# Two edge columns on ScalarE are tied behind the large copies beside them, in the spectral stage of a gated-mix gradient kernel

## The chip, the core and the metric

The kernel runs on one core of one Trainium2 chip. The metric is the device time of one execution in microseconds (us). Five engines work from queues of their own: PE (TensorE, matrix products), DVE (VectorE), ACT (ScalarE), POOL (GpSimd) and SP (SyncE, which here only starts transfers). ACT and POOL start transfers too. Every queue is worked off in the order in which it was written: an instruction that waits for a semaphore holds up all that stands behind it on its engine.

## What is computed

The reference, cut to what matters:

```python
g = sigmoid((x * gate_w).sum(-1, keepdims=True))
a = irfft2(rfft2(x) * (w_r + 1j * w_i), s=(S, D))      # spectral filter
r = relu(x @ w1 + b1);  b = (r * r) @ w2 + b2           # squared-ReLU layer
out = g * a + (1 - g) * b
```

with S = 2048 rows, D = 1024 columns and 3584 hidden units. Outputs are `out` and the gradients of everything but the second input, for a given `grad_out`: nine arrays. Two of them, `out_2` and `out_3`, are the gradients of the filter's real and imaginary part, 2048 x 513 each: 512 ordinary columns and one at the edge of the half spectrum.

## The kernel before, in words

Two streams of work are woven into one program. The first is the dense layer: `mlp_in` computes the hidden values (matrix products of lines L811 and L919) and, by `back_` and `grads`, the gradient at the hidden values (L818); `mlp_grads` then computes the weight gradients (L1241), and `Outputs` the output and the gradient of x (L1540). The second is the spectral filter: `first_stage`, `fft_mid` and `fft_out`. `spread` deals steps of the second stream between steps of the first, so PE gets an order in which both are mixed. A tile framework then orders the instructions of each engine by its own cost estimates and by the dependencies that it sees: instructions that touch the same elements stay in order, instructions that touch different elements of a tile may pass one another. `after(ins, earlier, NoSync)` adds a dependency by hand: `ins` must stand behind `earlier` on the same engine, without a semaphore.

The change lies in `fft_mid`, which runs from about 225 us to 615 us of the span. Its loop goes over m = 0 to 15; each m handles two of the 32 residue classes of the row index (64 rows each) in two halves of 256 columns, h = 1 first and then h = 0. In one m:

- `spectra` (L434): PE makes `px` for both halves from the loaded `z`.
- `transform` (L438 to L442): ACT copies `px` into the tile `x` (L439, 128x1024), writes its negative (L440, 128x512), and then writes one edge column of x from the small tile `ex` (L441, 128x6). The edge column is column 0 for h = 0, and column 256 for h = 1, behind the 256 that L439 and L440 write. After the h = 1 half, ACT starts four transfers of the next `z` (L404), tied behind L440.
- `products` (L449), `joined` (L454, L457, L461) and `grads_of_w` (L494, L495) on DVE: the filtered spectrum `y` and, in `gs`, the products for the filter's gradient.
- `rows_of` (L468, PE), `copy_of` (L475, ACT, into the single buffer `vc`) and `back` (L482, L483, DVE; stores to `y_scr` by L485 on POOL).
- `grads_out` for m - 1 (L498 to L508): for each half ACT scales `gs` into the bfloat16 tile `gw` (L499, 128x512, tied behind the second L440 of this m), and then one edge column of `gw` (L504, 128x2). That is column 0 for h = 0, and column 512 for h = 1. When both halves are written, POOL starts four stores of `gw` to `out_2` and `out_3` (L508). `gw` has one buffer: the first write into it for one m has to wait until the four stores of the m before have landed.

For h = 0 the edge column overlaps the columns of the large write, so it has always stood behind it. For h = 1 it lies beside them, and the framework was free to place L441 and L504 ahead of the large writes. In the order of the program before it does: L504 for h = 1 is placed as soon as `gs` is there, 9 to 27 us ahead of its L499, and it is there that the semaphores of the four stores are waited for.

On ACT the same queue holds the dense layer's work: copies of PSUM banks (L923), ReLU (L933, L936), squares (L786). PE cannot write the next product into a bank of `ph` before ACT's L923 or L933 (or DVE's L935) has read it, and cannot write `pd` before DVE's L822 has read it.

Of the kernel before, what the change touches and what calls it, by code (L numbers as in the profile page):

```python
# [21 lines left out]
def pair_of(m, R1):  # L22
    return (m, R1 - m) if m else (0, R1 // 2)
# [118 lines left out]
def kernel(  # L142
# [22 lines left out]
    nc = tc.nc  # L165
# [10 lines left out]
    Q, H, LW, W1 = D // 4, D // 2, g.Df + 1, g.Df  # L176
# [4 lines left out]
    GS = 2.0 / (S * D * XS * XS)  # L181
# [46 lines left out]
    HW, HL = H // 2, P // 2  # L228
# [21 lines left out]
    def after(ins, earlier, wait=mybir.DependencyClass.Sync):  # L250

        if earlier is not None:
            info = mybir.DependencyInfo(wait, mybir.DependencyReason.DATA)
            tc.add_manual_dep(ins.ins, earlier.ins.name, info, reason="paced")
# [78 lines left out]
    def fft_mid(filler):  # L333
# [103 lines left out]
        def transform(m, h, px, ex):  # L437
            x = fb.tile([P, 3, 2, WL], FDT, name="x", tag="x", bufs=2)  # L438
            nc.scalar.copy(out=x[:, 1:3, :, 0:HW], in_=px[:])  # L439
            copied = nc.scalar.mul(out=x[:, 0, :, 0:HW], in_=px[:, 1], mul=-1.0)  # L440
            nc.scalar.copy(out=x[:, :, :, h * HW], in_=ex[:, m, :, :, h])  # L441
            return x, copied  # L442

        def products(h, x, w):
# [53 lines left out]
        def grads_out(m, h, gs, gw, done):  # L498
            main = nc.scalar.mul(  # L499
                out=gw[:, :, h * HW : (h + 1) * HW].rearrange("p c (i g) -> p c i g", g=4),  # L500
                in_=gs[:, :, 0:HW].rearrange("p c (g i) -> p c i g", g=4), mul=GS,
            )
            after(main, done, mybir.DependencyClass.NoSync)
            nc.scalar.mul(out=gw[:, :, h * H], in_=gs[:, :, h * HW], mul=0.5 * GS)  # L504
            if h == 0:
                for c_, dst_w in enumerate((out_2, out_3)):
                    for n, k in enumerate(pair_of(m, R1)):
                        st(out=every(dst_w, k), in_=gw[lanes[n], c_, 0:W1])  # L508
# [8 lines left out]
        ex = edges_through(ams)  # L517
# [5 lines left out]
        x, y, gs, was = {}, {}, {}, None  # L523
        yield
        for m in range(NM):
            more = m + 1 < NM
            px = {h: spectra(m, pm[h]) for h in (1, 0)}
            if m:
                gs[0], _ = grads_of_w(0, x[0])
            x[1], copied = transform(m, 1, px[1], ex)  # L530
            if more:
                z = {h: inputs(m + 1, h, copied) for h in (1, 0)}
            yield
            x[0], done = transform(m, 0, px[0], ex)
            yield
            tt = products(1, x[1], w[1])
            if m:
                gw = fb.tile([P, 2, LW], BF16, name="gw", tag="gw")
                for h in (1, 0):
                    grads_out(m - 1, h, gs[h], gw, done)  # L540
# [31 lines left out]
        gw = fb.tile([P, 2, LW], BF16, name="gw", tag="gw")  # L572
        for h in (1, 0):
            pv = rows_of(NM - 1, y[h])
            vc = copy_of(NM - 1, pv)
            yield
            back(NM - 1, h, pv, vc)
            grads_out(NM - 1, h, gs[h], gw, vc[1])
            yield
# [1336 lines left out]
    out = later["out"]  # L1916
# [36 lines left out]
```

## Time and profile before

| | |
|---|---|
| median of 3 runs | 1206.56 us (1205.56 to 1207.74) |
| the profiled execution: its own time | 1211.84 us |
| the profiled execution: span from the first to the last instruction | 1210.1 us |
| PE busy in the span | 1176.1 us (97%) |
| DVE, ACT, POOL busy | 892.5 us (74%), 528.5 us (44%), 377.6 us (31%) |
| mean granted TensorE clock | 0.999 |
| from 250 to 465 us (215 us, the dense layer's first part beside `fft_mid`): PE, DVE, ACT busy | 197.11, 174.56, 142.24 us |
| from 500 to 600 us (weight gradients beside `fft_mid`): PE busy | 99.58 us |

"Busy" is the share of time in which an instruction of that engine ran; idle time that is put down to a releaser ("<-") is the time in which an engine's next instruction waited, and the releaser is what came last. The profile's own execution lies 5.28 us above the median of the timed runs, so differences are read within the profile and then carried to the median.

### The profile page before, as it was taken

The page shows a single profiled execution, that of the slowest core. Times are in us where ns is not written, and L with a number is a line of the kernel's source. Part 1 is how long each engine was busy: PE and PEld are TensorE (multiplying, and loading weights), DVE is VectorE, ACT ScalarE, POOL GpSimd, SP SyncE. Part 2 cuts the span into 40 slices and gives each one's busy share as a digit, 9 for nine tenths or more (in the row PEclk, how much of TensorE's full clock was granted, in tenths as well). Part 3 has the DMA queues.
Part 4 walks back from the last instruction along what each step waited for, and adds up shares of the span by engine and source line. Part 5 has one row for each costly group of instructions (what it writes and reads, how often), then busy time and mean ns, then how long its engine had stood idle before and what let it go on. Part 6 is the DMA issues. An engine that isn't in the chain of part 4 may idle for free.

```text
span 1210.1 us, 19414 instructions
## 1 busy us (share of the span) xinstructions
PE 1176.1 (97%) x7181; PEld 639.9 (53%) x7275; DVE 892.5 (74%) x1598; ACT 528.5 (44%) x961; POOL 377.6 (31%) x618
## 2 busy tenths in 40 slices
PE   9999999998989989999999999999999999999998
PEld 5555555443433333444445999999644444444444
DVE  6888887778878776877546666766786577986757
ACT  5668788586666674344322666665201010000000
POOL 0233443656656764455241223231101100000000
PEclk9999999999999999999999999999999999999999
DMA  9997675796868677889998999994788999664530
GB/s 277 268 304 210 190 203 161 211 236 155 216 156 200 223 189 221 177 181 228 217 198 167 207 244 227 266 236 150 238 177 243 256 270 282 199 187 152 175 126 35
DMA packets 329464, 249.84 MB, mean 206 GB/s; under 512 B 187912, under 2 KB 287658, under 8 KB 328858
## 3 DMA queue, kind: packets, MB, share of 16 engines
q1 hardware_dynamic: 268352, 112.12, 43.8%
q0 software_dynamic: 35136, 111.72, 29.4%
q10 hardware_dynamic: 25882, 24.76, 6.9%
q8 instruction: 57, 0.93, 0.3%
q14 instruction: 37, 0.30, 0.1%
HBM read 114.82 MB, written 89.67 MB: 169 GB/s over the span
## 4 chain that ended last, share of the span: by engine, by line
PE 69%; DVE 14%; ACT 6%; DMA 5%; issue 4%; POOL 1%; ACTq 1%; another core or an unknown queue 0%; SPq 0%; DVEq 0%; POOLq 0%
PE pX L1241 15%; PE xX L1540 13%; PE pV L1241 11%; PE pd L818 7%; PE xV L1540 6%; PE ph L919 5%; PE xZ L1540 3%; DMA out_dram<-gw 3%; PE pui L325 1%; DMA dhT_scr<-dhT 1%; DVE dhT L822 1%; PE pki L626 1%; ACT gw L499 1%; DVE rT L935 1%; PE pu L325 1%
## 5 line engine op out<-in xcount | busy, mean ns | idle before, releaser
L818 PE MATMUL pd<-dbT,w2T 128*128 128x512 bf16 x860 | 208.4, 380 | 7.5 <-DVE dhT L822 5.3
L818 PEld LDWEIGHTS <-w2T 128*128 128x128 bf16 x896 | 86.3, 98 | 109.5 <-issue 10.6
L822 DVE SCALAR_TENSOR_TENSOR dhT<-pd,rT 128x512 bf16<-128x512 f32 x112 | 76.7, 685 | 46.9 <-PE pd L818 43.0
L1540 PEld LDWEIGHTS <-dS 128*128 128x128 f16 x686 | 66.4, 98 | 79.4 <-issue 3.7
L1591 POOL DMA_DIRECT2D out_dram<-ot x32 | 17.3, 542 | 244.6 <-DVE ot L1647 128.0
L1657 ACT ACTIVATE w2br<-w2br,dsc 128x512 f32<-128x512 bf16 x8 | 5.8, 723 | 175.6 <-DVE ot L1647 117.4
L1540 PE MATMUL xX<-oT,dS 128*128 128x512 f16 x336 | 76.4, 379 | 0.6 <-DVE eR L1569 0.5
L1257 ACT COPY u<-pX 128x512 f32<-128x512 f32 x56 | 32.8, 585 | 95.7 <-PE pX L1241 89.8
L1540 PEld LDWEIGHTS <-odd 128*128 128x128 bf16 (+1 forms) x462 | 44.8, 98 | 51.5 <-issue 0.9
L1540 PEld LDWEIGHTS <-even 128*128 128x128 bf16 (+1 forms) x448 | 43.6, 98 | 52.6 <-issue 0.7
L1241 PEld LDWEIGHTS <-T 128*128 128x128 f16 x672 | 64.6, 98 | 7.5 <-issue 0.2
L485 POOL DMA_DIRECT2D y_scr<-pc x64 | 46.1, 722 | 65.5 <-DVE pc L482 44.0
L936 ACT ACTIVATE rT<-rT 128x512 bf16<-128x512 bf16 x69 | 43.4, 630 | 37.7 <-DVE rT L935 37.6
L786 ACT ACTIVATE h2T<-rT 128x1024 bf16<-128x1024 bf16 x56 | 59.5, 1063 | 0.2
L1261 DVE TENSOR_TENSOR whi<-pV,u 128x512 bf16<-128x512 f32 x28 | 19.3, 689 | 48.4 <-ACT u L1257 48.3
L1241 PEld LDWEIGHTS <-S 128*128 128x128 f16 x336 | 32.6, 98 | 40.5 <-DVE S L1173 1.9
L449 DVE TENSOR_TENSOR tt<-x,w 128x1028 f16<-128x1028 f16 (+1 forms) x64 | 42.1, 689 | 7.3 <-ACT x L439 3.5
L1241 PEld LDWEIGHTS <-resL 128*128 128x128 bf16 x448 | 43.0, 98 | 4.9
L1241 PEld LDWEIGHTS <-resR 128*128 128x128 f16 (+1 forms) x448 | 42.9, 98 | 4.9 <-issue 0.2
L1261 DVE TENSOR_TENSOR wlo<-pV,u 128x512 bf16<-128x512 f32 x28 | 19.2, 686 | 34.4 <-PE pV L1241 34.2
L919 PEld LDWEIGHTS <-w1g 128*128 128x128 bf16 x252 | 23.9, 98 | 37.8 <-issue 11.9
L1241 PEld LDWEIGHTS <-even 128*128 128x128 bf16 (+1 forms) x256 | 24.5, 98 | 32.7 <-issue 2.1
(382 smaller groups left out, 2782.3 us busy)
## 6 DMA issues: line engine op xcount, KB each, us to landing
h2T_scr<-h2T POOLq DMA_DIRECT2D x28, 512.0 KB, 4.6
dhT_scr<-dhT POOLq DMA_DIRECT2D x28, 512.0 KB, 4.6
y_scr<-pc POOLq DMA_DIRECT2D x64, 128.0 KB, 4.4
ax_scr<-yo POOLq DMA_DIRECT2D x16, 512.0 KB, 5.3
out_dram<-ot POOLq DMA_DIRECT2D x31, 256.0 KB, 3.4
z<-z_scr ACTq DMA_DIRECT2D x60, 128.0 KB, 4.3
out_dram<-whi POOLq DMA_DIRECT2D x28, 256.0 KB, 5.4
out_dram<-wlo POOLq DMA_DIRECT2D x28, 256.0 KB, 5.2
```

The costliest lines, as they stand in the source:

```text
L325: first_ = mm(pu[:, bank, lo : lo + n], lhsT=ft[:, b, :], rhs=mat[:, o : o + n], start=bool(f_ & 1), stop=bool(f_ & 2), skip_group_check=True,
L449: V(out=tt[:, k, :, :, 0:W], in0=x[:, a : a + 2, :, 0:W], in1=by, op=ALU.mult)
L485: st(out=columns_of(y_scr, c, h), in_=pc[:, n])
L786: after(nc.scalar.activation(h2T, rT, ACT.Square), behind_, mybir.DependencyClass.NoSync)
L818: mm(pd[:], lhsT=w_[:, ec, fc % FGC * P : (fc % FGC + 1) * P], rhs=dbT[:, ec, ss], start=(ec == 0), stop=(ec == DC - 1),)
L822: return STT(out=dhT, in0=pd[:], scalar=2.0, in1=rT, op0=ALU.mult, op1=ALU.mult, accum_out=gb1part[:, fc, sb : sb + 1],)
L919: mm(acc[:], lhsT=lhs[:, t, :], rhs=rhs[:, t, :], start=start and t == 0, stop=t == KH - 1, skip_group_check=True)
L936: nc.scalar.activation(rT, rT, ACT.Relu)
L1241: self.mm = mm(out, lhsT=lhs[:, t, m * P : (m + 1) * P], rhs=rhs[:, t, :], start=start and t + a == 0, stop=t == KH - 1, skip_group_check= ...
L1257: turn["ACT"] = nc.scalar.copy(out=t_[:], in_=self.X[:])
L1261: turn["DVE"] = self.added = V(out=self.half(row, j), in0=self.sums(acc), in1=self.sums(t_), op=ALU.add)
L1540: ins = mm(acc, lhsT=lhs[:, fc, :], rhs=rhs[:, fc, :], start=start and fc == 0, stop=fc == KH - 1 and bias is None, skip_group_check=True,)
```

## The change

Two dependencies are added, both within ACT and without a semaphore. The edge column of x stands behind the two large copies of x of the same half (L439, L440), and the edge column of `gw` stands behind the large write of `gw` of the same half (L499). No instruction is added or taken away, and no shape, buffer or transfer changes.

```diff
             copied = nc.scalar.mul(out=x[:, 0, :, 0:HW], in_=px[:, 1], mul=-1.0)
-            nc.scalar.copy(out=x[:, :, :, h * HW], in_=ex[:, m, :, :, h])
+            after(nc.scalar.copy(out=x[:, :, :, h * HW], in_=ex[:, m, :, :, h]), copied, mybir.DependencyClass.NoSync)
             return x, copied
...
             after(main, done, mybir.DependencyClass.NoSync)
-            nc.scalar.mul(out=gw[:, :, h * H], in_=gs[:, :, h * HW], mul=0.5 * GS)
+            edge_ = nc.scalar.mul(out=gw[:, :, h * H], in_=gs[:, :, h * HW], mul=0.5 * GS)
+            after(edge_, main, mybir.DependencyClass.NoSync)
             if h == 0:
```

The line numbers here and below are those of the kernel before; in the kernel after, every line from L505 on is one higher.

In the order of the built program the h = 1 column of x moves behind its L440 and ahead of the four starts of `z` (L404); the h = 1 column of `gw` moves behind its L499, and the wait for the four stores moves with the tile's first write to that L499. As the framework orders anew around them, some neighbours change places: on DVE, `y` (L454) and the ReLU's sum (L935) swap in several m, and `pc` (L482, L483) moves up; on ACT, in three of the m, the second copy into `vc` (L475) moves from behind L933 to ahead of it. PE's order changes in a few places by a few products; POOL's stores keep their order but for small moves, and SP's queue is unchanged.

## The prediction

> **What bounds the kernel now.** I read first the page's busy times with the slices, then the windows of 10 us over the stage that the change touches, then the waits of ACT and PE in that stage, and last the timelines of ACT and PE around single gaps.
>
> ```profile
> PE 1176.1 (97%) x7181; PEld 639.9 (53%) x7275; DVE 892.5 (74%) x1598; ACT 528.5 (44%) x961; POOL 377.6 (31%) x618
> PE   9999999998989989999999999999999999999998
> ```
>
> PE bounds the kernel: 1176.1 of 1210.1 us. All that an edit of order can win is in the 34.0 us in which PE is idle, and the slices below 9 put most of that in the third of the span where `fft_mid` runs beside the dense layer. The windows give it as numbers (columns: PE, PEld, DVE, ACT, POOL busy, then clock, DMA share and GB/s):
>
> ```profile
> 300.00:310.00 10.00, 7.32 (x38) 3.14 (x38) 8.08 (x14) 5.64 (x10) 3.79 (x5) 1.00 1.09 241
> 350.00:360.00 10.00, 7.87 (x33) 3.02 (x29) 6.76 (x15) 6.71 (x11) 6.23 (x10) 0.83 0.65 145
> 510.00:520.00 10.00, 9.95 (x51) 4.26 (x50) 8.38 (x16) 3.04 (x7) 4.29 (x8) 1.00 1.00 184
> ```
>
> From 250 to 465 us PE is busy for 197.11 of 215 us, so 17.9 us are idle. From 490 us on, beside the weight gradients, every window has 9.95 or 10.00: there `fft_mid` goes on and nothing is to be won. So the change is worth what it does between 250 and 465 us. Next, who made ACT and PE wait between 225 and 625 us (total us, times, longest):
>
> ```profile
> ACT gw L504 <- DMA out_dram<-gw: 32.1, 12, 4.2
> ACT gw L504 <- DVE pm L425: 5.2, 2, 3.3
> ACT gw L504 <- DVE pc L483: 3.4, 1, 3.4
> ...
> PE pd L818 <- DVE dhT L822: 5.3, 5, 2.1
> PE ph L919 <- ACT rT L933: 4.7, 2, 2.7
> PE ph L919 <- ACT cu L923: 3.1, 2, 1.9
> PE ph L919 <- ACT u L923: 2.0, 2, 1.2
> ```
>
> ACT stands still at the early edge column of `gw` 15 times, once for every m that has a predecessor: 32.1 + 5.2 + 3.4 = 40.7 us. The two DVE names are, I think, the same thing: at 321.00 `gs` had been ready since 316.7, while the four stores were started from 316.25 to 318.35 and land within 2.4 to 8.3 us. The timelines of ACT and PE show what one such stop does:
>
> ```profile
> 297.44 0.63 ACT L936 ACTIVATE rT<-rT 128x512 bf16<-128x512 bf16 x1 [0.63 <-DVE rT L935]
> 302.11 0.21 ACT L504 ACTIVATE gw<-gs 128x2 bf16<-128x2 f16 x1 [4.05 <-DMA out_dram<-gw]
> 302.22 0.57 ACT L475 COPY vc<-pv 128x512 f32<-128x512 f32 x1
> 302.69 0.69 ACT L933 ACTIVATE rT<-ph,b1col 128x512 bf16<-128x512 f32 x1
> ...
> 299.94 0.81 PE L919 MATMUL pZ<-xT,w1g 128*128 128x512 bf16 x3
> 303.43 1.02 PE L919 MATMUL ph<-xT,w1g 128*128 128x512 bf16 x4 [2.68 <-ACT rT L933]
> ```
>
> A write of two columns waits 4.05 us for the stores of the old `gw`. Behind it stands L933, which frees a bank of `ph`; PE has run out of other work and waits 2.68 us.
>
> **The change, part by part.** (1) The wait for the stores moves to the h = 1 L499. That L499 starts 9.15 us (466.60 against 457.45) to 27 us after the moment at which L504 was released before, so the stores have long landed: the wait costs nothing there, unless the stage gets 9 us shorter per m, out of some 23. Of the 15 stops, four lie in 500 to 600 us at full PE and one (479.65) at the start of the next part, behind which PE waits for DVE sums; these I count at nothing.
>
> Direct gain: the gaps that PE itself puts on what stands right behind an L504: 2.68 (303.43), 1.20 (346.69), 1.91 (390.31), 1.99 (436.68), and 0.22 (458.29, on L812) = 8.00 us. Is something else late there? At 303.43 the last product that L933 reads ends at 299.24; L475 ahead of it needs `pc`, done at 298.86 to 298.94. So L933 could end near 300.1, before PE ends its other work at 300.9. At 346.69 and 390.31, L923 follows at once; at 436.68, L933 ends near 433.7 and PE's other work at 434.7. I count 8.00 in full.
>
> Indirect gain: gaps on DVE's `dhT`, 5.3, and one of 0.40 on DVE's `rT`. Of these the 1.05 at 289.29 has no idle DVE ahead of it and stays. The other 0.50 + 2.07 + 0.34 + 0.40 + 1.34 = 4.65 each follow a stretch in which DVE works without a pause after having waited for ACT's L923 behind an L504 (idle 1.31 at 322.23, 2.19 at 346.67, 3.00 at 390.29, 1.73 at 413.65): DVE is late because ACT was. Each idle is longer than the gap it leads to. But DVE is busy for 174.56 of 215 us and takes a new order, so it is next in line: I take half, 2.3, with 0 and 4.65 as ends.
>
> Clock: in the 350 to 360 us window the clock is 0.83. The windows of 2 us inside show 0.64 and 0.51 from 356 to 360, after the 2.07 us gap. That costs 10 x 0.17 = 1.7 us. If that gap shrinks, some of it goes: half, 0.85, ends 0 and 1.7. After the longer gap at 303.43 the windows show 1.00. [...]
>
> (2) The h = 1 edge columns take their place in the run of large copies. Starts of neighbours (292.84 and 292.93 around an L441, 294.40 and 294.51 around an L504) give 0.10 us each. They are the same 32 instructions as before, so ACT's sum stays; but now they stand ahead of the L923 for which PE waits twice (0.79 and 1.23, "ACT u"): -0.2 us. One ACT wait goes, 2.1 us on L441 at 476.60; PE is full there, 0.
>
> (3) L441 now stands ahead of the four starts of `z` and of the next L439. What it does to a DMA start the trace can't show: from 0 to 0.5 us each (the longest idle of L439 put on "issue"), 7.5 us of ACT in 15 m. The loads land in 4.3 us and were issued at 286 to 288; DVE takes them up at 294.9, so they have about 3 us to spare. For PE I take 0, since only the "ACT u" chains could pass it on; the bad end is two of those, -1.
>
> (4) New neighbours. In three m the second L475 now stands ahead of L933 and must wait until DVE has read `vc` (L483). Its stops so far are 5.1 us in 5 at most 1.5 each; the longest L475 stop at all is 4.0. So 0 to 12 us on ACT. DVE's order has L483 higher up too, by about 3 us at 319.58, so I take 0 for PE. For the bad end: the four stops of 4.05, 3.65, 3.22 and 4.00 on ACT above gave 7.78 of PE gap, about half, so -6. `y` ahead of the ReLU's sum costs DVE's `rT` 0.69 each, but that sum waits for ACT's L923 anyway: 0. The few swaps on PE change no count, and POOL's stores of `gw` wait for the h = 0 column, which moves by a few small instructions only: 0.
>
> Sum: 8.00 + 2.3 + 0.85 - 0.2 = 10.95, so 11 us. The profiled execution goes from 1211.84 to about 1200.9; the median has 0.9956 of the profiled time, so 1206.56 - 10.9 = **1195.6 us**.
>
> **The rivals.** *More comes back.* DVE and the clock in full (14.2 net), and the gaps of 2.0 on "ACT u" and of 1.05 go too because DVE is early: about 17 us, 1189.5. For it: every link starts at the same stop. Against it: DVE's 81% in this part.
>
> *The wait comes back elsewhere.* The second L475 in three m stops ACT ahead of L933, -6, and DVE keeps its gaps: 8.0 - 6 - 0.2 - 1 = about 1 to 6 us gained, near 1203. For it: one buffer of `vc`, and DVE between the copies. Against it: `pc` moved up on DVE by more than the stop is long.
>
> *Nothing.* The wait of L499 is a real one, because the stores are late, or PE's gaps come from the weave and only change name: 1206.5. Against it: 9 us of room, and gaps that end within 1.4 us of the end of a stop.
>
> *Slower: the clock.* Where PE's short pauses fall into a bad place the clock is halved for some 3.4 us, which costs 1.7 us each time (356 to 360 us). The trace has one such event among the gaps of 250 to 465 us. If the new order spreads pauses so that more of them trip it, it wipes out the gain of 11 from 7 events on and makes the kernel slower by over 0.2% (2.4 us) from 8 on: 9 events give 1211. For it: a gap of 2.07 was enough once. Against it: 2.68 was not, and pauses get fewer. [...]
>
> **How the numbers follow.** Forecast (7 to 14 us gained) 0.60; more 0.14; the wait comes back (2.4 to 7) 0.13; nothing 0.07; slower 0.06. A measurement of this kernel can tell about 0.2%, 2.4 us, from no change. Faster: 0.60 + 0.14 + 0.13 - 0.01 = 0.86; same 0.08; slower 0.06. The range runs from 1188.5 (the first rival with a little more) to 1204 (the bad ends of (3) and (4)).
>
> **What would show it.** Right: L504 has no DMA wait left, and L499 none over 1 us; PE's waits on L933 and L923 `cu` fall from 7.8 to below 1.5; PE idle from 250 us to the end of the dense layer's part falls from 17.9 to 7 or so; the clock stays at 1.00 in the windows between; from there on every row of PE is as before, only earlier. Wrong: the same idle under another name (L475 on `pc`, `pd` on `dhT`), more windows under 1.00, or idle PE in 490 to 860 us, which would say that the next part was held by loads and gave the time back.

## The result, and the profile after

| | before | after |
|---|---|---|
| median (lowest to highest, runs) | 1207.15 us (1205.56 to 1211.33, 6) | 1199.36 us (1198.55 to 1203.24, 6) |
| the profiled execution (the slowest of each kernel): its own time, its span | 1211.84, 1210.1 us | 1203.24, 1201.2 us |
| mean granted TensorE clock of the profiled execution | 0.999 | 1.000 |

The ratio of the times is 0.9937, 95% interval 0.9916 to 0.9957; by the medians 7.8 us are gained, where 10.9 were forecast. (The ratios here and below are taken over all runs and are not exactly the quotients of the medians.) Two later sessions with the same kernel gave 0.9921 (0.9902 to 0.9941) and 0.9925 (0.9902 to 0.9948), that is 1207.64 - 1199.29 = 8.4 us and 1207.61 - 1199.13 = 8.5 us.

From here on, line numbers from L505 on are one higher in the kernels that have the tie on `gw` (L923 is L924, L933 is L934, and so on). First the page of the kernel after, its busy times and its slices:

```profile
PE 1180.0 (98%) x7275; PEld 640.2 (53%) x7275; DVE 891.3 (74%) x1598; ACT 528.7 (44%) x961; POOL 379.8 (32%) x618
PE   8999999999989999999999999999999999999998
```

The three 8s that the slices of before showed between 272 and 454 us have become one (an 8 in the first slice, far ahead of the stage, is new). The 3.9 us by which PE is busier are no more work: the trace of before lacks 94 matmul records (x7181 against x7275). So I do not compare busy times but the moments at which stages begin. Where each stage starts is read from the timelines: the first product of L434 (`fft_mid`), of the weight gradients (L1241), of the gradient of x (L1540).

| us | before | after | after, second trace (experiment 5) | after, third trace (experiment 10) |
|---|---|---|---|---|
| up to the first `px` product | 226.0 | 225.8 | 224.1 | 224.7 |
| from there to the weight gradients | 247.8 | 238.8 | 237.1 | 236.1 |
| weight gradients | 382.1 | 382.0 | 382.1 | 382.1 |
| from there to the end | 354.2 | 354.6 | 353.8 | 353.8 |

All of the gain lies in the stage that the change touches, and the stages after it give nothing back. The windows (columns as in the prediction; the first line is of the kernel before, the others of the kernel after) say the same:

```profile
250.00:465.00 215.00, 197.11 (x940) 83.28 (x957) 174.56 (x373) 142.24 (x257) 131.22 (x205) 0.99 0.76 199
250.00:460.00 210.00, 200.60 (x976) 85.02 (x976) 175.36 (x377) 146.98 (x264) 135.68 (x209) 1.00 0.82 207
300.00:310.00 10.00, 10.00 (x51) 4.30 (x49) 9.76 (x20) 7.10 (x12) 5.91 (x9) 1.00 1.08 202
350.00:360.00 10.00, 7.86 (x38) 3.12 (x37) 7.52 (x19) 8.57 (x16) 5.54 (x11) 1.00 0.84 197
510.00:520.00 10.00, 10.00 (x51) 4.30 (x49) 8.62 (x13) 2.56 (x5) 5.84 (x8) 1.00 0.87 196
```

PE is idle for 9.4 us of 210, where it was idle for 17.9 of 215 (17 of the missing records of before lie there, 940 against 957; at 3.9 us for 94 that is about 0.7 us of the 17.9, an estimate). The window with the 2.68 us gap is full now, and 350 to 360 us still has 2.14 us without PE, but at full clock instead of 0.83. Last, the waits of ACT and PE between 225 and 625 us:

```profile
ACT vc L475 <- DVE pc L483: 9.6, 10, 1.5
...
PE ph L920 <- ACT u L924: 3.3, 3, 1.3
PE pd L819 <- DVE dhT L823: 3.2, 4, 1.1
...
PE pd L819 <- DVE rT L936: 1.0, 1, 1.0
PE ph L920 <- ACT rT L934: 0.9, 2, 0.7
PE ph L812 <- ACT rT L934: 0.6, 1, 0.6
```

No row is left in which ACT waits on L504 or on L499 for a store: 40.7 us of stops are gone. On PE the rows "ACT rT" and "ACT cu", 4.7 + 3.1 + 0.2 = 8.0 us before, have shrunk to 0.9 + 0.6 = 1.5. But the wait of `vc` on `pc` has grown from 5.1 us in 5 to 9.6 in 10, and "ACT u" from 2.0 to 3.3. A timeline of ACT around the new 0.70 us gap on PE shows the first of the two:

```profile
380.36 0.58 ACT L475 COPY vc<-pv 128x512 f32<-128x512 f32 x1 [0.64 <-DVE pc L483]
380.84 0.69 ACT L934 ACTIVATE rT<-ph,b1col 128x512 bf16<-128x512 f32 x1
```

```profile
379.86 1.03 PE L920 MATMUL pZ<-xT,w1g 128*128 128x512 bf16 x4
381.58 1.02 PE L920 MATMUL ph<-xT,w1g 128*128 128x512 bf16 x4 [0.70 <-ACT rT L934]
```

The second L475 of this m stands ahead of L934 and waits 0.64 us for DVE to read the one buffer of `vc`. L934 frees the bank of `ph` 0.70 us too late for PE. This is the pattern of the old stop with a shorter wait.

### The profile page after: what moved, and what is told of

It is laid out like the page before. It is cut to its first block, busy times and chain, and to the rows that moved or that the text cites. A ratio compares the mean times of both kernels' runs of the same rounds, so it can differ in the third digit from the quotient of the medians.

```text
span 1201.2 us, 19492 instructions
## 1 busy us (share of the span) xinstructions
PE 1180.0 (98%) x7275; PEld 640.2 (53%) x7275; DVE 891.3 (74%) x1598; ACT 528.7 (44%) x961; POOL 379.8 (32%) x618
## 4 chain that ended last, share of the span: by engine, by line
PE 71%; DVE 11%; DMA 8%; ACT 5%; issue 3%; POOL 1%; SPq 1%; ACTq 0%; DVEq 0%; POOLq 0%
PE pX L1242 16%; PE pV L1242 11%; PE pd L819 10%; PE xX L1541 10%; PE ph L920 6%; PE xV L1541 5%; PE xZ L1541 3%; DMA w2left<-in_B_w_dram 2%; DMA w1r_scr<-w2left 2%; PE ph L812 2%; PE pui L325 1%; PE pki L627 1%; DMA odd<-h2T_scr 1%; ACT gw L499 1%; PE pu L325 1%
## 5 line engine op out<-in xcount | busy, mean ns | idle before, releaser
L819 PE MATMUL pd<-dbT,w2T 128*128 128x512 bf16 x896 | 211.4, 379 | 4.7 <-DVE dhT L823 3.2
L819 PEld LDWEIGHTS <-w2T 128*128 128x128 bf16 x896 | 86.2, 98 | 108.5 <-issue 9.7
L509 POOL DMA_DIRECT2D out_dram<-gw x64 | 33.8, 534 | 35.5 <-ACT gw L504 25.0
```

Source lines behind the costliest of these rows:

```text
L819: mm(pd[:], lhsT=w_[:, ec, fc % FGC * P : (fc % FGC + 1) * P], rhs=dbT[:, ec, ss], start=(ec == 0), stop=(ec == DC - 1),)
```

## The experiments

The theory: the early L504 carried the wait for the four stores, and taking that wait away gives the whole gain; the tie in x gives none. The rivals: the place of the edge columns counts, whatever they wait for; or the new order of DVE and ACT does it. A second question is where the missing 3 us of the forecast are. Each kernel was timed beside the kernel before on the same chip.

### 1. The tie on gw alone

```diff
-            nc.scalar.mul(out=gw[:, :, h * H], in_=gs[:, :, h * HW], mul=0.5 * GS)
+            edge_ = nc.scalar.mul(out=gw[:, :, h * H], in_=gs[:, :, h * HW], mul=0.5 * GS)
+            after(edge_, main, mybir.DependencyClass.NoSync)
```

> Only the edge column of gw is tied behind its large write; the edge column of x stays free as in the kernel before. Theory W (the whole gain is the wait for the four stores of gw, which leaves the early L504): about -8 us against the kernel before, ratio 0.993, no ACT wait on L504. In its built order the second copy into vc (L475) stays behind the ReLU copy in the three m where the full change moves it ahead; if those three places cost what the trace of after shows (0.20 + 0.70 + 0.60 = 1.5 us on PE), this kernel gains 1 to 2 us more than the full change: -9 to -10. Rival P (the gain comes from the new order of x and its neighbours): 0 to -3.

Measured: 1198.05 us against 1206.6; ratio 0.9916 (0.9903 to 0.9929). The stage takes 235.9 us. Its PE and ACT waits:

```profile
PE ph L920 <- ACT u L924: 4.2, 4, 1.3
PE pd L819 <- DVE dhT L823: 2.6, 2, 1.5
...
ACT vc L475 <- DVE pc L483: 7.7, 7, 1.5
```

The whole gain is there with this tie alone, and PE no longer waits for ACT's `rT` at all. In this kernel's order the second L475 stays behind L934 in the three m; so it is the tie in x that moves it.

### 2. The tie in x alone

```diff
-            nc.scalar.copy(out=x[:, :, :, h * HW], in_=ex[:, m, :, :, h])
+            after(nc.scalar.copy(out=x[:, :, :, h * HW], in_=ex[:, m, :, :, h]), copied, mybir.DependencyClass.NoSync)
```

> Only the edge column of x is tied behind the large copies of x; the edge column of gw keeps its early place and its wait for the stores. Theory W: no gain, the 15 stops at the gw column are still there with some 40 us on ACT; and since the second vc copy now stands ahead of the ReLU copy in three m, 0 to +3 us. Rival P: -5 to -8.

Measured: 1210.83 us against 1206.6; ratio 1.0029 (1.0012 to 1.0047), a little slower. The stage takes 248.6 us. The timelines of ACT and PE around its longest gap (this kernel has the line numbers of before):

```profile
386.58 0.63 ACT L936 ACTIVATE rT<-rT 128x512 bf16<-128x512 bf16 x1 [2.05 <-DVE rT L935]
391.26 0.21 ACT L504 ACTIVATE gw<-gs 128x2 bf16<-128x2 f16 x1 [4.05 <-DMA out_dram<-gw]
391.38 0.57 ACT L923 COPY u<-ph 128x512 f32<-128x512 f32 x1
```

```profile
386.81 1.67 PE L818 MATMUL pd<-dbT,w2T 128*128 128x512 bf16 x7
391.99 1.86 PE L919 MATMUL ph<-dbn,Sw 128*128 128x512 f16 x4 [3.51 <-ACT u L923]
```

The stop on L504 is still there, 4.05 us long, with L923 behind it, and PE waits 3.51 us: longer than any of its gaps on ACT in the kernel before (2.68). In the window from 390 to 400 us the clock falls to 0.83. So the tie in x does nothing against the stop, and by itself it costs 1.4 to 5.7 us (0.12 to 0.47% of 1206.6). That loss goes with the clock: the seven of its 12 runs at a mean clock of 0.997 took 1210.43 to 1216.68 us, the two at 1.000 took 1204.68 and 1208.01, on either side of the 1206.22 us in the middle of the runs of before at 1.000.

### 3. The edge column early, but without the wait

The h = 1 edge column is written early, as before, but into a tile of its own with two buffers; a small copy brings it into `gw` behind the large write. Nothing is tied in x. That is 16 small ACT instructions more.

```diff
-            nc.scalar.mul(out=gw[:, :, h * H], in_=gs[:, :, h * HW], mul=0.5 * GS)
+            if h:
+                ge = fb.tile([P, 2], BF16, name="ge", tag="ge", bufs=2)
+                nc.scalar.mul(out=ge[:], in_=gs[:, :, h * HW], mul=0.5 * GS)
+                after(nc.scalar.copy(out=gw[:, :, h * H], in_=ge[:]), main, mybir.DependencyClass.NoSync)
+            else:
+                nc.scalar.mul(out=gw[:, :, h * H], in_=gs[:, :, h * HW], mul=0.5 * GS)
```

> The early edge write keeps its early place and goes into a tile of its own (two columns, two buffers), so that it waits for no store; one more ACT copy of two columns per m, tied behind the large write, brings it into gw. Nothing is tied in x. Theory W: the gain is there although the place is the early one: -7 to -10, less 16 copies of 0.1 us on ACT. A rival by which the early place itself costs (it stands ahead of work that PE needs and waits for gs on DVE): -3 or less, with ACT waits of over 10 us on the early write put down to DVE.

Measured: 1200.49 us against 1206.6; ratio 0.994 (0.9924 to 0.9956). The profiled execution begins some 5 us later (230.3 us up to the first `px` product, with a pause of PE between 20 and 40 us and a clock of 0.91 there), but the stage itself takes 234.4 us, 13.4 less than before. In the medians 6.1 us are gained, a little under the 7 to 10 that were expected. The waits of ACT's early write in the stage:

```profile
ACT ge L506 <- DVE gs L495: 4.8, 5, 1.5
```

The early write is still there and waits only for its own data, 1.5 us at most. The gain comes without moving the edge column: it is the wait for the stores that counted, not the place.

### 4. The kernel after with two buffers for vc

`vc` becomes 16 bits wide, so that two buffers fit where one was; that rounds a value on the way.

```diff
-            vc = fb.tile([P, 2, HW], FP32, name="vc", tag="vc")
+            vc = fb.tile([P, 2, HW], FDT, name="vc", tag="vc", bufs=2)
```

> The full change, and vc in two buffers (in 16 bits instead of 32, so that two fit where one was; this rounds a middle value of the filter's output). It takes away the stop of the second vc copy on DVE's pc: 9.6 us on ACT, 10 times, in the trace of after. If that stop is the cause of PE's three waits on the ReLU copy (1.5 us): -1 to -3 us against the full change, so -9 to -11 against before, ratio about 0.991. If the stop is covered: the same as the full change, -7 to -8.

Measured: 1199.3 us against 1206.6; ratio 0.9938 (0.9924 to 0.9952). The row "vc L475 <- DVE pc" is gone, and so are PE's waits for ACT's `rT`. The stage takes 236.2 us against 238.8, 237.1 and 236.1 of the kernel after. The median gains nothing by it. Of the two readings set down beforehand it is the second that came: taking the stop away makes the kernel no faster, so the waits it removes are seen in the trace, but no price of theirs is.

### 5. The kernel after, a second time

No edit: it stands beside the next three kernels on the same chip.

> The full change once more, beside the kernels of this group on one chip. Theory V (the tie of x costs 2 to 3 us, since it moves the second vc copy ahead of the ReLU copy in three m): -7 to -8.5 against before, and the part of the trace from the first product of px to the first of the weight gradients near 238.8 us. Rival R (the tie of x costs nothing, and the 2.5 us between the full change and the gw tie alone are the difference of two sessions): about -10 here.

Measured: 1199.29 us against 1207.64; ratio 0.9921 (0.9902 to 0.9941). The stage takes 237.1 us. By the medians 8.4 us are gained, which lies in theory V's range; but the interval (7.1 to 11.8 us) holds rival R's 10 as well, so this run alone does not decide.

### 6. The tie on gw alone, with two buffers for vc

The edits of 1 and 4 together.

> Only the gw tie, and vc in two 16-bit buffers. Theory V: with the second vc copy behind the ReLU copy in those three m anyway, its stop on pc (7.7 us on ACT in the gw tie alone) holds up little that PE needs: the stage takes 234 to 236.5 us, -10 to -11 against before. If the remaining stops on pc feed PE's gaps: 232 to 234 us, -12 to -14.

Measured: 1196.85 us against 1207.64, ratio 0.9905 (0.9884 to 0.9926), and 2.4 us below the kernel after on the same chip. The stage takes 233.7 us; what PE still waits for there is "ACT u", 3.3 us, and DVE's `dhT` and `rT`, 2.1 + 0.4 us. This is the lowest median of the study, below both kernels. Against 1198.05 and 1197.96 us of the same kernel with one buffer (experiments 1 and 9, other sessions), the second buffer is worth about 1 us, which the scatter between sessions does not confirm. The time lies in the range of the first reading and the stage in that of the second, so the run does not decide between them.

### 7. The tie on gw alone, and all of the gw writes later

The writes of `gw` for m - 1 are queued behind the first copy into `vc` of this m, so that the run of large writes no longer stands ahead of L924.

```diff
-                for h in (1, 0):
-                    grads_out(m - 1, h, gs[h], gw, done)
...
+                for h in (1, 0):
+                    grads_out(m - 1, h, gs[h], gw, vc[1] or done)
```

> Only the gw tie, and the two large writes of gw are moved behind the first vc copy of the same m, so that they no longer stand ahead of the copy into u (L924), for which PE waits 4.2 us in four m when only gw is tied. If those two writes (2 x 1.0 us, plus 0.2) are what u is late by: PE's waits on u fall below 1 us, the stage goes from 235.9 to 232 or 233 us, -12 to -14 against before. If u is late because the ReLU copies ahead of it wait for DVE: 235 to 236 us, -10. The stores of gw start some 3 us later; should they bind again, ACT waits of L499 on the stores appear.

Measured: 1202.27 us (1195.46 to 1214.28, 12 runs) against 1207.64; ratio 0.9945 (0.9918 to 0.9971). "ACT u" on PE falls to 1.9 us (from 4.2 in experiment 1), not below 1, and 1.2 us of waits for ACT's `rT` are there again; the stage falls to 233.6, and the profiled execution is with 1195.46 us the fastest of its runs. But its runs scatter with their clock: 1195.46, 1197.05 and 1200.79 us at 1.000, 1201.92 to 1205.98 at 0.997, 1208.71 and 1208.85 at 0.994, 1214.28 at 0.991. That is about 2 us for each 0.001. The one fall in the trace of before (3.41 us at half clock in 1210, so 0.0014 of the mean clock, for 1.7 us) would give 1.2 of these 2 us, an estimate; the rest would be the pauses. No trace shows the pauses of those longer runs, so what starts them is open, and the median gains 5.4 us where 12 to 14 or 10 were expected.

### 8. The same with two buffers for vc

The edits of 4 and 7 together.

> The gw tie, the late large writes and the two 16-bit vc buffers together. If both kinds of stop reach PE: 230 to 232 us for the stage, -13 to -16 against before. If DVE (83% busy in this stage) is the bound behind them: no better than the late writes alone, within 1 us.

Measured: 1205.02 us against 1207.64; ratio 0.9982 (0.9962 to 1.0001). The stage takes 242.8 us, 9.2 more than in experiment 7, which neither reading foresaw, and PE waits 6.7 us for DVE's `rT`. The timelines of DVE, and of PE behind it:

```profile
320.09 0.42 DVE L425 TENSOR_TENSOR pm<-z 128x512 f16<-128x512 f16 x1 [4.00 <-DMA z<-z_scr]
...
322.58 0.74 DVE L936 SCALAR_TENSOR_TENSOR rT<-pZ,b1col,cu 128x512 bf16<-128x512 f32 x1
```

```profile
323.38 3.14 PE L819 MATMUL pd<-dbT,w2T 128*128 128x512 bf16 x8 [4.67 <-DVE rT L936]
...
388.30 3.20 PE L819 MATMUL pd<-dbT,w2T 128*128 128x512 bf16 x8 [2.02 <-DVE rT L936]
```

DVE waits 4.00 us for a load of `z`, and 1.40 us for the next one behind it. L936, which needs nothing of `z`, stands behind both in the queue, and PE waits 4.67 us for it. After both pauses L819's x8 takes 3.14 and 3.20 us; in the kernel after the same x8 took 1.89 us at full clock. It is the pattern of the stop that the change removed, on another engine: an in-order queue stands still for a transfer and holds back work that has nothing to do with it. Why the load came so late was not followed further.

### 9 and 10. The tie in x, priced on one chip

No new edit: the kernel of experiment 1 and the kernel after, side by side.

> The same kernel as e1: only the edge column of gw is tied behind its large write, nothing in x. It stands on the same chip as e10, which has both ties, so that the tie in x is priced directly. Theory 'the tie in x costs something, because it draws the second L475 ahead of L933 in three m': from the first px product to the first weight-gradient product about 236 us, 1.2 to 3 us less than e10, no wait of PE on rT of the second L933, and the timed median 1 to 2.5 us below e10. Rival 'the tie in x is free': both medians within 0.5 us of each other.

> The changed kernel with both ties, beside e9 on the same chip. Theory 'the tie in x costs': the stage about 237 to 239 us, with PE waiting for rT on ScalarE at both the recomputation's and the backward's first product of an m (0.6 to 0.9 us each in sum), and the median 1 to 2.5 us above e9. Rival 'free': no difference beyond 0.5 us, and the waits on rT balanced by shorter waits elsewhere.

Measured: 1197.96 us (1196.31 to 1199.91) with the tie on `gw` alone, 1199.13 us (1198.81 to 1202.23) with both, against 1207.61. The stages take 234.8 and 236.1 us. In the profile with both ties PE waits for ACT's `rT` again 0.7 and 0.6 us; with one tie it does not. So the tie in x costs 1.2 us in the medians and 1.3 us in the traces. The scatter of the six runs each overlaps, but over all sessions the 18 runs with both ties have their middle at 1199.23 us and the 11 with one tie at 1198.05. The first theory holds in its size, at the lower end; the stage with both ties is shorter than its 237 to 239 us.

By what way the tie costs this is not shown. The two waits add up to the same 1.3 us, but others are shorter in their place: all of PE's waits between 225 and 465 us are 7.1 us with both ties and 6.8 with one. Experiment 4 has both ties and no stop of L475, and is no faster; experiment 6, which differs from it only by the tie in x, takes 1196.85 us against 1199.3 (in another session). PE's own work speaks for a second way. In all five traces with the tie in x two of the groups of eight `pv` products (L468) are split into one and seven, and the 84 products of that line in the stage keep PE busy for 11.8 to 11.9 us; in the seven traces without it they are not split and take 10.9 to 11.1. No run changes that order alone.

## Why the prediction was right, and where its size was off

The time forecast was 1195.6 us, and 1199.36 came: the mechanism and the side held, the gain is 7.8 to 8.5 us by the medians where 10.9 were expected. Two signs of being right were missed narrowly: PE's idle time from 250 us on fell to 9.4 us and not to 7 or so, and its waits on L933 and `cu` to 1.5 us and not below.

**The stop itself (step 1).** Shown. ACT's stops for the four stores are gone from L504, and L499 has none in their place, as the 9 us of room said. Experiment 3 leaves the write early and has the gain too, so it is the wait. The rival "nothing" falls with the result itself, and the tie in x earns nothing by itself (experiment 2).

**The direct gain, 8.00 us.** All five gaps ended, as counted. But 1.5 us of waits on the same releaser came back in other places, by step (4).

**The new neighbours (step 4).** "I take 0 for PE" did not hold. The second L475 ahead of L933 in three m did stop ACT (9.6 us instead of 5.1) and did pass on to PE: the stop is 0.63 or 0.64 us in each of the three (at 315.19, 380.36 and 441.10 us), and the gaps on PE behind them are 0.20, 0.70 and 0.60 us. The kernel with the tie in x is 1.2 us slower than the one without, measured side by side. That these stops are what costs it is not shown: without them the kernel with both ties is no faster (experiment 4), and PE's order changed as well (experiments 9 and 10). The rival "the wait comes back elsewhere" had the right place and too high a price of 6: the stops are 0.64 us, not 4. I had argued from one place that DVE's `pc` moves up by more than the stop is long; in the run it was late by 0.64 us in all three.

**The indirect gain on DVE, 2.3 us.** PE's waits for DVE's `dhT` and `rT` went from 5.3 + 0.4 to 3.2 + 1.0 in the first trace, and to 2.4 in the third: 1.5 to 3.3 us gained. Half of what was available was about right; the half was the middle of two ends, so its fit is partly luck.

**"ACT u" (step 2), -0.2 us.** Wrong in sign: these waits grew from 2.0 to 3.3 us. They also grew without the tie in x (4.2 and 3.4 us in the two traces of that kernel), so the two columns that step (2) moved are not what does it. A timeline of ACT in the kernel after shows what stands ahead:

```profile
416.24 0.99 ACT L439 CAST x<-px 128x1024 f16<-128x1024 f32 x1
417.13 0.60 ACT L440 ACTIVATE x<-px 128x512 f16<-128x512 f32 x1
417.62 1.10 ACT L499 ACTIVATE gw<-gs 128x512 bf16<-128x512 f16 x1
...
418.80 1.09 ACT L499 ACTIVATE gw<-gs 128x512 bf16<-128x512 f16 x1
419.78 0.58 ACT L924 COPY u<-ph 128x512 f32<-128x512 f32 x1
```

```profile
420.41 1.02 PE L920 MATMUL ph<-xT,Sw 128*128 128x512 f16 x4 [1.31 <-ACT u L924]
```

Four large writes and two edge columns in a row, 3.5 us without a pause (416.24 to 419.78), and then the copy that PE waits 1.31 us for. With the store waits gone, this run of copies is the next thing that is late here. I had asked what is late next for the direct gaps one by one, but not for the stage. Experiment 7, which moves the L499 pair away, takes the row down to 1.9 us, so the pair is a part of it and not the whole.

**The clock, 0.85 us (ends 0 and 1.7).** In the traces the event after 354 us is gone, the whole 1.7 us. In the medians a second view tells more: 51 timed runs of the kernel before have a mean clock of 0.994 to 1.000, and their time goes with it: 1206.22 us in the middle of the 11 runs at 1.000, 1210.09 in that of the 7 at 0.997. 17 of the 18 runs of the kernel after are at 1.000. The median of all 51 is 1207.53, so by these medians about 1.3 us of the gain are clock, and about 7.0 (1206.22 to 1199.2) are order. That the forecast's half lies close to this is luck: it was the middle of two ends, without a reason for either. The length of a pause alone did not decide the clock here: x8 products took 3.20 us instead of 1.89 after a pause of 2.02 us (experiment 8), while the pause of 2.68 us in the kernel before was followed by a full clock (1.00 in the windows of 2 us from 302 to 308). What else decided it is not shown; the last section lists cases from the traces.

**The start of z (step 3), 0.** Right for this change: DVE waits for `z` 2.2 us in two places and PE for none of it. The room is small, though: in experiment 8 one load came 4.00 us late, and PE stood still for it.

**The slower rival, the clock.** The change does not have it. Its relatives do: the clock is 0.997 in the profiles of experiments 2 and 8 and down to 0.991 in runs of 7, and 2 did end slower than before.

**What stays open.** The tie in x accounts for 1.2 of the missing 2.4 to 3.1 us, and "ACT u" for about 1.3 to 1.5 in the traces. But the trace from which I took the gaps belonged to an execution of 1211.84 us, 5.28 above its median and above every one of the 17 timed runs with its mean clock of 0.999 (1205.84 to 1209.30). I carried the difference over by a factor of 0.9956, which takes off only 0.05 us. If part of those 5.28 us was idle PE in this very stage, the usual run had less to gain; the stages of 247.8 us against 236.1 to 238.8 (9.0 to 11.7 us) beside medians that differ by 7.8 to 8.5 speak for that. An estimate from the record goes the same way: the 17 runs at 0.999 have a span of 1205.7 us in the middle, and the parts outside the stage take 960.0 to 962.4 us in the ten traces without a fall of the clock there, which leaves 243.3 to 245.7 us for the stage, 2.1 to 4.5 less than in the trace that I read. That alone could be the missing 2.4 to 3.1 us. No trace of an execution of before near the median exists, so it isn't shown.

## What to carry to other kernels

When a large tile has one buffer and is stored by DMA, the first write into it carries the wait for the old stores, however small that write is (here one of 128x2, which waited up to 4.2 us); look in the in-order engine's waits for a tiny instruction with a DMA behind its arrow, and put it behind the work that others wait for. A hand-made order should tie no more than that: the tie in x here had no wait to remove, the order around it changed on ACT, DVE and PE, and the kernel with it is 1.2 us slower. And take the gaps from an execution near the median, or take the excess off the gain.

## What the runs showed of the hardware that was not expected

- PE's clock fell at pauses of 2.02, 2.07, 3.00, 3.51 and 4.67 us and in a window with 4.51 us of idle PE, and not at one of 2.68 us. In the trace of before the stretch at half clock (0.50) runs from 356.55 to 359.96 us; it is 3.41 us long and so costs about 1.7 us. The 0.83 over 10 us in experiments 2 and 8 comes to the same 1.7 us each time, an estimate.

| trace | PE's pause | granted clock (window, us) |
|---|---|---|
| experiment 8 | 4.67 us, up to 323.38 | 0.50 (324 to 326), 0.68 (326 to 328), 1.00 (328 to 330) |
| experiment 3 | 4.51 us in all, between 20 and 40 | 0.91 (20 to 40) |
| experiment 2 | 3.51 us, up to 391.99 | 0.75 (391 to 393), 0.50 (393 to 395), 0.89 (395 to 397) |
| experiment 2 | 3.00 us, up to 484.87 | 0.83 (480 to 490) |
| before | 2.68 us, up to 303.43 | 1.00 (302 to 304, 304 to 306, 306 to 308) |
| before | 2.07 us, up to 356.32 | 0.64 (356 to 358), 0.51 (358 to 360) |
| experiment 8 | 2.02 us, up to 388.30 | 0.79 (388 to 396) |
| before | 1.99 us, up to 436.68 | 1.00 (430 to 440, 440 to 450) |
| experiment 2 | 1.94 us, up to 423.74 | 1.00 (420 to 430, 430 to 440) |
| before | 1.91 us, up to 390.31 | 1.00 (390 to 400) |

  The order by length does not hold: the clock stayed full at 2.68 us and fell at 2.07 and 2.02. What decided beside the length is not shown; no run moved a pause to test it.
- Between runs of one kernel the mean clock varied from 0.994 to 1.000 (before) and from 0.991 to 1.000 (experiment 7), 19 us of time in the latter.
- POOL's starts of transfers stood still as well. In experiment 2 it was idle for 4.54 us, by its timeline for the load of another tile, before it started the last two stores of `gw`; ACT's stop for them ended at 391.26, 5.9 us after that start. How late a store lands was set in part by what stood ahead of its start:

```profile
385.37 1.13 POOL L508 DMA_DIRECT2D out_dram<-gw  x2 [4.54 <-DMA wn<-in_A_w_r_dram]
```
